# Three MLPs as half products inside the attention groups of the next query block

## The chip, the cores and the metric

The kernel runs on one core of a Trainium2 chip. The metric is the device time of one execution in microseconds (us), the median of several runs; lower is better. The core's engines work beside each other and wait for one another by semaphores: PE multiplies matrices (PEld is its loading of weights, which may lie beside a matmul), DVE (VectorE), ACT (ScalarE) and POOL (GpSimd) work elementwise, and SP issues transfers (DMA).

## The reference

One transformer layer, 2048 rows of 512 features, 32 heads of 16, and an MLP with 1792 hidden features, all in float32:

```python
def _A_ref(x, wqkv, wo):
    ...
    scores = jnp.einsum("bhqd,bhkd->bhqk", q, k) * scale
    p = _softmax(scores, axis=-1)
    o = jnp.einsum("bhqk,bhkd->bhqd", p, v)
    return (lambda x, *d: x.transpose(*d))(o, 0, 2, 1, 3).reshape(B, S, D) @ wo

def _B_ref(x, w1, w2):
    h = jnp.einsum("bsd,df->bsf", x, w1)
    h = _silu(h)
    out = jnp.einsum("bsf,fd->bsd", h, w2)
    return out

x = A_x
h = x + _A_ref(_layernorm(x, axis=-1), A_wqkv, A_wo)
h2 = h + _B_ref(_layernorm(h, axis=-1), B_w1, B_w2)
```

## The kernel before

Products are made in halves of precision: an operand is split into a high and a low fp16 part, and each product is three matmuls (high x high, low x high, high x low). So a first MLP product for 128 hidden features and 512 rows is 12 matmuls (4 chunks of features by 3), and the second product of 128 rows is 42 (14 chunks of hidden features by 3).

The 2048 queries are worked in four query blocks of 512, and a block in eight items of four heads each, so there are 32 items. An item has 16 groups, one for each 128 keys: 512 groups in all, numbered g in the main loop (L1347). A group makes four score matmuls, one for each head, of 128 keys by 512 queries; an operand is 64 rows deep, 48 of features in three parts and 16 that subtract the row's maximum. Two of the four heads lie on the upper 64 rows of the PE's array and two on the lower 64, so a matmul on one half can run beside one on the other. `scores` (L462) puts each result through the exponential on ACT into an SBUF tile. `values` (L856) multiplies the exponentials of a group with the values, four heads beside each other in float32, two groups behind (`LAG`), and adds them up in one bank of PSUM over the 16 groups; then the sum is copied out (`finish_item`, L874).

The maximum of a row must be known before the scores of its item begin. `maximum` (L285) makes a matmul of 128 queries by 512 keys, 48 rows deep, and a reduce on DVE; an item needs 64 of them, the kernel 2048. `maxima` (L1324) decides how many of them stand in a group, by how far ahead the next items' maxima are due and by a most of three, and the loop puts each behind a score of the other half. `singles` and `burst` (L443, L438) put them elsewhere: three amid an output product, and six or four at a time, as pairs of banks with one reduce for two, between the products of an MLP.

PSUM has eight banks. In attention, four are for scores (`st`), three for single maxima (`sm`), used in turn, and one for the values.

After the last item of a query block come its output product and normalization (`output`, L1184), in the second half of the item that follows, and then, ahead of the second item (`marks`), the whole MLP (`finish_block` and `mlp`, L1204 and L1118): 14 first products of 12 whole matmuls, each through SiLU on ACT, and then the second products. This is done for the first three query blocks. The last block's MLP comes at the end (`finish_last`).

What sets the order: every engine's instructions keep the order in which the program issues them, and transfers are issued by SP in that order too.

Of the kernel before, what the change touches and what calls it, by code (L numbers as in the profile page):

```python
# [20 lines left out]
P = 128  # L21
# [22 lines left out]
SPLIT = 12  # L44
MX = 2.0 ** 15
# [3 lines left out]
PTS = 16  # L49

EARLY = 8
# [13 lines left out]
WAIT = 2  # L65
JOINT = 2
AHEAD = 4
# [4 lines left out]
BESIDE = (138, 138, 110)  # L72
OUTPUT = 8

# [16 lines left out]
def attention_mlp_kernel(ctx: ExitStack, tc: tile.TileContext, x, wqkv, wo, w1, w2, out):  # L91
# [5 lines left out]
    def mm(*a, **k):  # L97
        tc.keep_in_program_order(nc.tensor.matmul(*a, **k))  # L98
# [12 lines left out]
    def act(fn, *a, **k):  # L111
        pin(getattr(nc.scalar, fn)(*a, **k))  # L112
# [80 lines left out]
    factors = const.tile([P, 14], F32, name="factors")  # L193
    sigma, inverse = factors[:, :4], factors[:, 4:8]
    w1_s, w2_s, wo_s, o_s = (sigma[:, n:n + 1] for n in range(4))
    h_f, g_s, out_f, wo_f, o_minus, o_twice = (factors[:, n:n + 1] for n in range(8, 14))
# [141 lines left out]
    def place_far(piece):  # L338
# [4 lines left out]
        issue = dma_beside if at["beside"] else dma  # L343
# [27 lines left out]
    at = {"item": 0, "done": 0, "half": 0, "step": 0, "due": 0, "attention": False, "group": None, "ready": 0, "next": 0, "blocks": True, "beside": False}  # L371
# [21 lines left out]
    def found_maxima(piece):  # L393
        g = at["group"]
        marked = g is not None and g + 1 in marks
        if g is None or marked or piece[1] is None and start_of(piece) - g > FAR:
            soon(WAIT + 1 if g is None or marked else CALM, place_far, piece)
            finish_max(piece, marked)
            return
# [55 lines left out]
    pts, den, pools = {}, {}, []  # L455
    taken = iter(range(10 ** 6))

    def pt_tile(name, dtype=F32):
        pool_of = pools[next(taken) % PTS >= EARLY]
        return pool_of.tile([P, 512], dtype, tag="pt", name=name)  # L460

    def scores(g, k, kind="st"):  # L462
# [7 lines left out]
        pts[g, k] = pt_tile("pt")  # L470
        act("activation", pts[g, k], ps, AF.Exp, scale=qk_f)


    with ExitStack() as pa:
        pb = pa.enter_context(ExitStack())
        lay_out(sm=range(5), st=range(5, 8))
        wp = pa.enter_context(tc.tile_pool(name="wp", bufs=1))
        wvp = pb.enter_context(tc.tile_pool(name="wvp", bufs=1, side="right"))
        xp = pa.enter_context(tc.tile_pool(name="xp", bufs=3))
# [34 lines left out]
        def square_rest(u):  # L514

            n = u - 7
            if 0 <= n < len(pieces):
                square_into(staged[n % 2], staged[n % 2], n)
# [931 lines left out]
```

## Time and profile before

| | us |
|---|---|
| time, median of 3 runs | 1593.08 (1592.78 to 1593.82) |
| span of the profiled execution | 1591.2 |
| PE busy | 1579.5 |
| DVE busy | 1386.9 |
| ACT busy | 1205.0 |
| POOL busy | 484.8 |

The profiled execution is listed with its span, the time from its first instruction to its last; its own time is not listed beside the runs, and the median of the runs is 1.9 us above the span. Times in rows count from the start of the span. The ends of matmuls are modelled: a matmul of 512 columns is listed with 0.38 us, though the next may start 0.22 us later, so starts are read and not ends. The granted clock of the PE is 1.00 in all of the stretches, which is its upper level (2.4 GHz).

### The profile page before, as it was taken

The numbers are of one execution on the slowest core, as the hardware profiler recorded it, in microseconds if no ns is written. First come the engines' busy times: TensorE is split into PE (matmuls) and PEld (weight loads), VectorE is DVE, ScalarE is ACT, GpSimd is POOL, SyncE is SP. The second block draws the span as 40 slices with busy tenths as digits, with TensorE's granted clock in tenths as the row PEclk, the third lists the DMA queues.
The fourth block names the chain that finished last, engine by engine and source line by source line (L and its number), as shares of the span: only waits on it lengthen the run. The fifth ranks groups of instructions, "written<-read, shape, count | busy, mean of one in ns | idle before, by whom it ended". The sixth has DMA issues, their size and how long they took to land. (4 is left out here: it accounts for less than half of the span.)

```text
span 1591.2 us, 28420 instructions
## 1 busy us (share of the span) xinstructions
PE 1579.5 (99%) x10476; PEld 471.7 (30%) x10476; DVE 1386.9 (87%) x2045; ACT 1205.0 (76%) x2384; POOL 484.8 (30%) x764
## 2 busy tenths in 40 slices
PE   9999999999999999999999999999999999999999
PEld 6434222222223322222224322222224322222254
DVE  7999999999998889999988889999986889998432
ACT  6545799999964179999973179999974189999732
POOL 5643544544446101211146101211146101211200
PEclk9999999999999999999999999999999999999999
DMA  6667533443443511121243521112143511100232
GB/s 216 174 177 221 136 86 91 113 119 86 116 100 102 157 47 35 38 51 44 50 102 101 152 53 34 39 41 53 48 104 108 159 40 37 34 12 22 74 87 73
DMA packets 124099, 140.29 MB, mean 88 GB/s; under 512 B 41808, under 2 KB 78736, under 8 KB 123960
## 3 DMA queue, kind: packets, MB, share of 16 engines
q1 hardware_dynamic: 117744, 128.34, 30.5%
q10 hardware_dynamic: 6216, 10.15, 2.3%
q8 instruction: 82, 1.34, 0.4%
q14 instruction: 57, 0.47, 0.1%
HBM read 104.68 MB, written 24.85 MB: 81 GB/s over the span
## 5 line engine op out<-in xcount | busy, mean ns | idle before, releaser
L112 ACT ACTIVATE pt<-ps 128x512 f32<-128x512 f32 x2048 | 1009.3, 611 | 154.4 <-PE ps L98 154.0
L301 DVE TENSOR_REDUCE mx<-ps 128x1 f32<-128x512 f32 x1470 | 925.1, 684 | 48.2 <-PE ps L98 20.3
L98 PE MATMUL ps<-pt,va 128*17 128x512 f32 x4096 | 537.5, 598 | 1.1
L98 PE MATMUL ps<-qs,ks 64*128 64x512 f16 x2048 | 530.9, 379 | 1.5 <-DMA qs<-mn 0.4
L98 PE MATMUL ps<-ks,qs 48*128 48x512 f16 x2048 | 495.4, 380 | 2.6 <-ACT pvs L112 1.1
L299 DVE TENSOR_REDUCE mx<-ps 128x2 f32<-128x1024 f32 x289 | 334.9, 1219 | 43.8 <-PE ps L98 42.5
L98 PEld LDWEIGHTS <-ks 64*128 64x128 f16 x2048 | 149.3, 95 | 549.2 <-issue 432.5
L105 POOL TENSOR_TENSOR ri<-rc,minus 128x16 f32<-128x16 f32 x31 | 90.7, 2926 | 242.5 <-DMA rc<-dn 192.3
L98 PE MATMUL ps<-w,gh 128*128 128x512 f16 (+1 forms) x678 | 154.4, 378 | 0.0
L98 PE MATMUL ps<-hts,w 128*128 128x512 f16 (+1 forms) x708 | 153.3, 369 | 0.0
L98 PEld LDWEIGHTS <-qs 48*128 48x128 f16 x2048 | 126.1, 94 | 77.5 <-issue 61.3
L98 PEld LDWEIGHTS ps<-pt,va 128*17 128x17 f32 x4096 | 69.0, 95 | 225.7 <-issue 205.4
L112 ACT ACTIVATE g<-ps,factors 128x512 f32<-128x512 f32 x56 | 38.4, 686 | 125.0 <-PE ps L98 95.7
L105 POOL TENSOR_TENSOR mx<-mx 128x32 f32<-128x32 f32 x52 | 12.6, 241 | 386.4 <-DVE mx L301 379.8
L98 PEld LDWEIGHTS <-w 128*128 128x128 f16 x708 | 66.5, 98 | 78.6 <-issue 10.2
L98 PEld LDWEIGHTS <-gh 128*128 128x128 f16 x678 | 63.1, 98 | 82.9 <-issue 13.7
L112 ACT ACTIVATE ks<-ps 128x512 f32<-128x512 f32 x30 | 17.9, 598 | 50.5 <-PE ps L98 45.1
L115 DVE SCALAR_TENSOR_TENSOR gh<-g,factors,gh 128x512 f16<-128x512 f32 x14 | 10.5, 751 | 52.1 <-ACT gh L112 52.1
L105 POOL TENSOR_TENSOR sl<-ks,sh 128x512 f16<-128x512 f32 x30 | 34.7, 1157 | 51.5 <-ACT sh L112 38.1
L105 POOL TENSOR_TENSOR gh<-g,gh 128x512 f16<-128x512 f32 x42 | 48.6, 1156 | 3.5
L105 POOL TENSOR_TENSOR ot<-ot,den 128x512 f32<-128x512 f32 (+1 forms) x16 | 20.4, 1273 | 84.4 <-DMA den<-dr 75.8
L98 PE MATMUL ps<-xth,wqk_h 128*128 128x512 f16 x120 | 45.8, 381 | 0.0
(155 smaller groups left out, 919.7 us busy)
## 6 DMA issues: line engine op xcount, KB each, us to landing
w<-w2d SPq DMA_DIRECT2D x98, 256.0 KB
ks<-kd SPq DMA_DIRECT2D x120, 192.0 KB
w<-w1d SPq DMA_DIRECT2D x56, 256.0 KB
ks<-in_B_w_dram ACTq DMA_DIRECT2D x28, 256.0 KB
w<-in_B_w_dram SPq DMA_DIRECT2D x28, 256.0 KB
qs<-qd SPq DMA_DIRECT2D x128, 48.0 KB
kd<-sh SPq DMA_DIRECT2D x16, 256.0 KB
qd<-sh SPq DMA_DIRECT2D x16, 256.0 KB
```

Of the source, the lines that this page charges most:

```text
L98: tc.keep_in_program_order(nc.tensor.matmul(*a, **k))
L105: tc.keep_in_program_order(getattr(nc.gpsimd, op)(*a, **k))
L112: pin(getattr(nc.scalar, fn)(*a, **k))
L115: pin(getattr(nc.vector, fn)(*a, **k))
L299: pin(nc.vector.tensor_reduce(of, space[:, n:n + 2, :], axis=AX.X, op=ALU.max))
L301: pin(nc.vector.tensor_reduce(of[:, j:j + 1], space[:, n, :], axis=AX.X, op=ALU.max))
```

## The change

The MLPs of the first three query blocks are no longer made in one piece. From the second group after a mark on, 112 groups (110 in the last of the three) each take a share of them. A matmul of 128 rows is cut into two of 64 rows, one on the upper and one on the lower half of the array, which add into one bank of PSUM (bank 3, taken from the scores, which keep three). A group makes six halves (seven in the last chain of some 14 groups) on one half of the array, and its four scores all on the other half: an even group makes the scores of two heads for itself and the next group, an odd group those of the other two heads for the group before and itself. Four groups make a first product, 14 a second product of 128 rows. A half product waits for the last exponential of the group before (`after`). In these groups the values are one group behind, and four maxima stand in a group (five or three where an item's maxima fall late); the SiLU is made from a tanh on ACT and four steps on POOL; the sum of the second product is scaled on ACT and added on POOL. The weights of the second product are loaded once for each 128 rows, so four times for a block.

Elsewhere, an ordinary group may have four maxima, the output product of each 128 rows has three maxima amid it in all blocks, and the values' sums are copied out by ACT from the second query block on. Bursts of pairs now stand only in the projections ahead of the loop.

```diff
--- before.py
+++ after.py
 SPLIT = 12
+SPACING = 4
 MX = 2.0 ** 15
 
 
 LAG = 2
-PTS = 16
-
-EARLY = 8
+PTS = 12
...
+AHEAD = 6
+
 JOINT = 2
-AHEAD = 4
+MORE = 3
 FAR = 8
 CALM = 4
 
 
-BESIDE = (138, 138, 110)
...
+LEAD = 7
...
-BURSTS_1 = ({f: 6 for f in range(FC) if f not in (6, 13)},) * 2 + ({f: 6 for f in range(FC) if f % 3 != 1},)
-BURSTS_2 = 12, 12, 10
-SPAN_2 = 12 * (FC - 2) - 3
-
-MORE = 2, 2, 0
...
+    def after(ins, earlier):
+
+        tc.add_manual_dep(ins.ins, earlier.ins.name, mybir.DependencyInfo(
+            mybir.DependencyClass.Sync, mybir.DependencyReason.DATA), reason="row halves in one bank")
...
 def scores(g, k, kind="st"):
...
-        pts[g, k] = pt_tile("pt")
-        act("activation", pts[g, k], ps, AF.Exp, scale=qk_f)
+        def weigh():
+            pts[g, k] = pt_tile("pt")
+            return act("activation", pts[g, k], ps, AF.Exp, scale=qk_f)
+
+        return weigh
...
-        elif i in FIRSTS:
+        elif i < FIRSTS[0]:
+            dve("tensor_copy", pvs, pv)
+        else:
             act("copy", pvs, pv)
-        else:
-            dve("tensor_copy", pvs, pv)
         if i == LAST:
...
-    def mlp(b):
...
+    weights_of = [*(("w1", f) for f in range(FC)), *(("w2", f) for _ in range(4) for f in range(FC))]
+    wanted = []
+
+    def want(n):
+        for _ in range(min(n, len(wanted))):
+            load_weights(*wanted.pop(0))
+
+    def take(kind, f):
+        want(1)
+        return ws.pop((kind, f))
+
+    def first_of(f):
+        w1h, w1l = (w.rearrange("p (c n) -> p c n", n=P) for w in take("w1", f))
+        for c in range(DC):
+            for w, x in ((w1h, hth), (w1l, hth), (w1h, htl)):
+                yield w[:, c, :], x[:, c, :]
+
+    def second_of(t):
+        rows = slice(t * P, (t + 1) * P)
         for f in range(FC):
-            tick()
-            next_weights()
-            w1h, w1l = (w.rearrange("p (c n) -> p c n", n=P) for w in ws.pop(("w1", f)))
-            ps = space[:, f % 2, :]
-            n = BURSTS_1[b].get(f, 0)
-            if f == 0:
-                burst(n, 4, 6, 2)
-                n = 0
-            weave(product(ps, lambda c: w1h[:, c, :], lambda c: w1l[:, c, :],
-                          lambda c: hth[:, c, :], lambda c: htl[:, c, :], DC),
-                  {6: lambda: burst(n, 4, 6, 2)} if n else {})
-            gates.append(gate(ps, "pool"))
-
-        act("activation", small.tile([P, 1], F32, name="sw"), ident[:, :1], AF.Exp)
-        acc = [space[:, n, :] for n in range(4)]
-        positions = {SPAN_2 * (n + 1) // BURSTS_2[b]: n for n in range(BURSTS_2[b])}
-
-        def insert(k):
-            half = 12 * FC // 2
-            pairs = (4, 6)
-            if not (half - 12 < k < half + 12 or k == SPAN_2):
-                pairs = (2 if k < half else 0), 4, 6
-            burst(2 * len(pairs), *pairs)
-
-        k = 0
-        for part in range(2):
-            for f in range(0, FC - 4 * part, 2):
-                at["beside"] = part == 0 or f < 4
-                tick()
-                next_weights()
-                next_weights()
-                for _ in pair_seconds(b, acc, (2 * part, 2 * part + 1), f, gates):
-                    k += 1
-                    if k in positions:
-                        insert(k)
-        for _ in range(2):
-            tick()
-            next_weights()
-            next_weights()
-
-        def scores_in(*ring):
-            lay_out(sm=ring)
-            some_scores(4)
-
-        last_seconds(b, acc, gates[-4:], {6: lambda: scores_in(0, 1, 4, 5), 18: lambda: scores_in(6, 7, 4, 5)}, (2, 3))
-        lay_out(sm=attention_banks[:3])
+            w2h, w2l = take("w2", f)
+            for side, w in ((0, w2h), (1, w2h), (0, w2l)):
+                yield gates[:, f, side, rows], w
+
+    def end_first(f, ps):
+        z = zp.tile([P, 512], F32, name="g")
+        act("mul", z, ps, h_f)
+
+        def bend():
+            t = zp.tile([P, 512], F32, name="t", tag="oh")
+            act("activation", t, z, AF.Tanh, scale=0.5)
+            pool("tensor_scalar", t, t, 1.0, g_half, op0=ALU.add, op1=ALU.mult)
+            pool("tensor_tensor", t, t, z, ALU.mult)
+            pool("tensor_copy", gates[:, f, 0], t)
+            low(gates[:, f, 1], t, gates[:, f, 0], "pool")
+
+        soon(2, bend)
...
+    def end_second(b, t, ps):
+        z = zp.tile([P, 512], F32, name="g")
+        act("mul", z, ps, out_f)
...
+    chains, current = [], {}
+
+    def begin_mlp(b):
+        chains.extend((3 * DC, 6, first_of(f), lambda ps, f=f: end_first(f, ps)) for f in range(FC))
+        chains.extend((3 * FC, 7 if 4 * b + t == KC - 5 else 6, second_of(t), lambda ps, t=t: end_second(b, t, ps)) for t in range(4))
+
+    def half_product(j):
+        if j == 0:
+            current["open"].append(next(current["of"]))
+        lhs, rhs = current["open"][current["half"][j] - current["gone"]]
+        if j:
+            current["open"].pop(0)
+            current["gone"] += 1
+        r = slice(64 * j, 64 * j + 64)
+        ins = mm(space[:, 3, :], lhs[r], rhs[r], start=current["half"] == [0, 0],
+                 stop=current["half"][1] == current["count"] - 1)
+        if "fence" in current:
+            after(ins, current.pop("fence"))
+        current["half"][j] += 1
+
+    def beside_products(g, n):
+
+        if not current:
+            count, share, of, end = chains.pop(0)
+            current.update(count=count, share=share, of=of, end=end, half=[0, 0], open=[], gone=0)
+        side = g % 2
+        heads = [(x, k) for x in (g - side, g - side + 1) for k in range(4) if head(x, k)[1] != side]
+        i, found, left = next_item(), [0, 0], [0, 0]
+        if i < ITEMS:
+            left = [len(todo[i, j]) for j in range(2)]
+        count = current["count"] - current["half"][0] if side == 0 else current["half"][0] - current["half"][1]
+        count = min(current["share"], count)
+        for _ in range(min(n, sum(left))):
+            j = 1 - side
+            if 4 + found[j] > count + found[side] or found[j] == left[j]:
+                j = side
+            if found[j] == left[j]:
+                j = 1 - j
+            found[j] += 1
+        other = [("max", 1 - side)] * found[1 - side]
+        other = [step for m, of in enumerate(heads) for step in [("score", of), *other[m:m + 1]]]
+        same = [("max", side)] * found[side]
+        same[1:1] = [("half", side)] * count
+        short = len(same) - len(other)
+        if short > 0:
+            other[-1:-1] = [("none", 0)] * short
+        waiting = []
+        for m in range(max(len(other), len(same))):
+            for kind, x in same[m:m + 1] + other[m:m + 1]:
+                if kind == "score":
+                    waiting.append(scores(*x))
+                    if len(waiting) < 4:
+                        waiting[-1]()
+                elif kind == "max":
+                    one_max(x)
+                elif kind == "half":
+                    half_product(x)
+        if current["half"][1] == current["count"]:
+            current["end"](space[:, 3, :])
+            current.clear()
+            waiting[3]()
+        else:
+            current["fence"] = waiting[3]()
...
-            weave(project_rows(n, ps), {6: lambda: singles(3)} if n < MORE[b] else {})
+            weave(project_rows(n, ps), {6: lambda: singles(MORE)})
...
-    def finish_block(b, pending):
-
-        act("activation", small.tile([P, 1], F32, name="sw"), ident[:, :1], AF.Silu)
-        load_weights("w1", 4)
-        for g in pending:
-            values(g)
-        mlp(b)
...
+    beside = {g for m in marks for g in range(m + 2, min(groups, m + 2 + 4 * FC + 4 * FC))}
+    fixed = {**{8 * KC * b + c: 3 + MORE * (OUTPUT < c <= OUTPUT + 4) for b in range(1, NB) for c in range(2, KC + 2)},
+             **{g: 4 for g in beside}}
+    before = [sum(n for x, n in fixed.items() if x < g) for g in range(groups + 1)]
+    free = [sum(x not in fixed for x in range(g)) for g in range(groups + 1)]
+
...
+        if g in beside:
+            at["due"] = 0
+            most = 4 - late_now + (64 + 4 * (g + LEAD) > at["done"])
+            return max(0, min(most, ready - at["done"]))
...
+        if g in fixed:
+            rate = 3
...
-        most = 2 if at["step"] in late or c == JOINT and i and i - 1 not in FIRSTS else 3
+        most = 2 if late_now or c == JOINT and 0 < i <= FIRSTS[0] else 4
...
-            finish_block(i // 8 - 1, (g - 2, g - 1))
+            begin_mlp(i // 8 - 1)
+        if (g in beside) != (g - 1 in beside):
+            lay_out(st=range(3 if g in beside else 4))
...
+        if g in beside:
+            beside_products(g, n)
+        else:
...
-        if g - LAG >= 0 and not (g in marks or g - 1 in marks):
-            values(g - LAG)
+        while done <= g - (1 if g in beside else LAG):
+            values(done)
+            done += 1
```

The rest of the diff: buffers change their pools and places (12 tiles for exponentials instead of 16, room for all gates of a block), the factors are computed in two parts, and finding a maximum that is far from due takes a path on POOL everywhere.

The order on the PE in a group of the third query block's items, before: `ks` and `qs` are keys and queries; a row that writes from `ks` with the weights `qs` is a maximum, one from `qs` with the weights `ks` a score; `pt,va` are values.

```order
L98 MATMUL ps<-pt,va 17x512 x4
L98 LDWEIGHTS ks_99
L98 MATMUL ps<-qs_100,ks_99 128x512
L98 LDWEIGHTS qs_106
L98 MATMUL ps<-ks_105,qs_106 128x512
L98 LDWEIGHTS ks_99
L98 MATMUL ps<-qs_100,ks_99 128x512
L98 LDWEIGHTS qs_106
L98 MATMUL ps<-ks_105,qs_106 128x512
L98 LDWEIGHTS ks_99
L98 MATMUL ps<-qs_100,ks_99 128x512
```

The start of a group beside the MLP in the changed kernel, in the same notation; `hts,w` is a half of a first product.

```order
L97 MATMUL ps<-pt,va 17x512 x4
L97 LDWEIGHTS qs_108
L97 MATMUL ps<-ks_107,qs_108 128x512
L97 LDWEIGHTS ks_105
L97 MATMUL ps<-qs_106,ks_105 128x512
L97 LDWEIGHTS w
L97 MATMUL ps<-hts,w 128x512
L97 LDWEIGHTS qs_108
L97 MATMUL ps<-ks_107,qs_108 128x512
L97 LDWEIGHTS w
L97 MATMUL ps<-hts,w 128x512
L97 LDWEIGHTS ks_105
```

Before, such a group is score, maximum, score, maximum, score, maximum, score. Now it is maximum, score, half, maximum, half, score, half, maximum, half, score, half, maximum, half, score: 14 matmuls between two values blocks instead of seven, and the whole products of the MLP stand nowhere else.

The end of a group near the beginning of the first query block, before, on the PE:

```order
L98 LDWEIGHTS ks_99
L98 MATMUL ps<-qs_100,ks_99 128x512
L98 LDWEIGHTS qs_106
L98 MATMUL ps<-ks_105,qs_106 128x512
L98 LDWEIGHTS ks_99
L98 MATMUL ps<-qs_100,ks_99 128x512
L98 MATMUL ps<-pt,va 17x512 x4
```

And the end of the same group in the changed kernel:

```order
L97 LDWEIGHTS ks_99
L97 MATMUL ps<-qs_100,ks_99 128x512
L97 LDWEIGHTS qs_106
L97 MATMUL ps<-ks_105,qs_106 128x512
L97 LDWEIGHTS ks_99
L97 MATMUL ps<-qs_100,ks_99 128x512
L97 LDWEIGHTS qs_106
L97 MATMUL ps<-ks_105,qs_106 128x512
L97 MATMUL ps<-pt,va 17x512 x4
```

A fourth maximum now stands behind the last score, ahead of the values. Of the 128 groups after the first, 30 have four maxima, 11 have two and 87 three; before, none has more than three.

## Rows read from the trace of the kernel before

**Rows 1.** The page: busy us, share of the span, instructions of each engine.
```profile
PE 1579.5 (99%) x10476; PEld 471.7 (30%) x10476; DVE 1386.9 (87%) x2045; ACT 1205.0 (76%) x2384; POOL 484.8 (30%) x764
```

**Rows 2.** Windows: stretch, length, busy PE PEld DVE ACT POOL (instructions), clock, DMA, GB/s.
```profile
179.40:431.80 252.40, 251.56 (x1913) 56.03 (x1912) 240.64 (x391) 251.99 (x515) 123.54 (x185) 1.00 0.41 108
431.80:472.60 40.80, 40.52 (x265) 10.81 (x267) 37.42 (x64) 30.47 (x62) 16.68 (x24) 1.00 0.42 84
472.60:571.20 98.60, 97.88 (x503) 37.77 (x498) 83.83 (x81) 28.00 (x44) 35.94 (x59) 1.00 0.42 119
571.20:791.10 219.90, 219.65 (x1674) 48.86 (x1673) 210.83 (x343) 219.79 (x449) 36.75 (x68) 1.00 0.19 44
791.10:1150.80 359.70, 358.19 (x2438) 97.51 (x2437) 332.42 (x486) 278.37 (x553) 87.95 (x145) 1.00 0.27 69
1150.80:1499.80 349.00, 347.36 (x2337) 94.61 (x2341) 288.49 (x431) 274.10 (x542) 87.06 (x139) 1.00 0.26 67
```

**Rows 3.** Timeline of the PE, one group: start us, duration, instruction, count.
```profile
701.84 0.39 PE L98 MATMUL ps<-qs,ks 64*128 64x512 f16 x1
701.84 0.60 PE L98 MATMUL ps<-ks,qs 48*128 48x512 f16 x2
...
702.50 0.38 PE L98 MATMUL ps<-qs,ks 64*128 64x512 f16 x1
702.81 1.05 PE L98 MATMUL ps<-pt,va 128*17 128x512 f32 x8
703.79 0.39 PE L98 MATMUL ps<-qs,ks 64*128 64x512 f16 x1
```

**Rows 4.** Timeline of ACT and DVE, the first exponential and reduce of that group.
```profile
702.26 0.60 ACT L112 ACTIVATE pt<-ps 128x512 f32<-128x512 f32 x1
...
702.29 0.69 DVE L301 TENSOR_REDUCE mx<-ps 128x1 f32<-128x512 f32 x1
```

**Rows 5.** Timeline of PE and DVE, a maximum that waits for its bank.
```profile
466.89 1.28 DVE L301 TENSOR_REDUCE mx<-ps 128x1 f32<-128x512 f32 x2
...
468.23 0.37 PE L98 MATMUL ps<-ks,qs 48*128 48x512 f16 x1
```

**Rows 6.** Timeline of the PE in the first MLP: bursts and first products.
```profile
479.17 0.82 PE L98 MATMUL ps<-ks,qs 48*128 48x512 f16 x6
479.93 2.76 PE L98 MATMUL ps<-hts,w 128*128 128x512 f16 x12
482.62 0.94 PE L98 MATMUL ps<-ks,qs 48*128 48x512 f16 x6
```

**Rows 7.** Timeline of the PE, the values behind three output groups.
```profile
449.35 1.05 PE L98 MATMUL ps<-pt,va 128*17 128x512 f32 x8
...
454.74 1.05 PE L98 MATMUL ps<-pt,va 128*17 128x512 f32 x8
...
459.48 1.05 PE L98 MATMUL ps<-pt,va 128*17 128x512 f32 x8
```

**Rows 8.** Timeline of the PE near the loop's end: values behind groups without maxima.
```profile
1479.45 1.05 PE L98 MATMUL ps<-pt,va 128*17 128x512 f32 x8
...
1481.41 1.05 PE L98 MATMUL ps<-pt,va 128*17 128x512 f32 x8
...
1498.08 2.77 PE L98 MATMUL ps<-pt,va 128*17 128x512 f32 x24
```

**Rows 9.** The page's groups: busy us, mean ns of one, idle before.
```profile
L301 DVE TENSOR_REDUCE mx<-ps 128x1 f32<-128x512 f32 x1470 | 925.1, 684 | 48.2 <-PE ps L98 20.3
...
L98 PEld LDWEIGHTS <-ks 64*128 64x128 f16 x2048 | 149.3, 95 | 549.2 <-issue 432.5
...
L112 ACT ACTIVATE g<-ps,factors 128x512 f32<-128x512 f32 x56 | 38.4, 686 | 125.0 <-PE ps L98 95.7
```

**Rows 10.** Windows, a stretch of the first MLP's second products, columns as above.
```profile
520.00:560.00 40.00, 39.82 (x203) 15.60 (x202) 35.43 (x34) 3.46 (x5) 5.32 (x8) 1.00 0.57 159
```

More of the change, by code (lines that the diff above doesn't have):

```diff
@@ L342, in place_far @@
         dve("transpose", mt, split.pop(piece))
-        issue = dma_beside if at["beside"] else dma
+        issue = dma
         for b in range(4):
@@ L370, in attention_mlp_kernel @@
     END = 64 * ITEMS
-    at = {"item": 0, "done": 0, "half": 0, "step": 0, "due": 0, "attention": False, "group": None, "ready": 0, "next": 0, "blocks": True, "beside": False}
+    at = {"item": 0, "done": 0, "half": 0, "step": 0, "due": 0, "attention": False, "group": None, "ready": 0, "next": 0, "blocks": True}
     agenda, late = {}, {}
@@ new lines, in idle, with turn_high @@
+    def idle(n):
+        ps = bank()
+        for c in range(n):
+            tr(ps[:, columns(c % 4)], ident, ident)
+    def turn_high(b, t):
+        ps = bank("sm").rearrange("p (c n) -> p c n", n=P)
+        high = xth[b] if b else xth0
+        for c in range(4):
+            tr(ps[:, c, :], xts[b][:, t, c * P:(c + 1) * P], ident)
+        act("copy", high[:, :, columns(t)], ps)
+        return ps
+    idle(20)
+    found = [statistics(xts[0][:, t, :], LN) for t in range(2)]
+    turned, ps_vs = [], []
@@ new lines, in first_rows, with first_products @@
+    def first_rows(t):
+        normalize(xts[0][:, t, :], xts[0][:, t, :], *found[t])
+        turned.append(turn_high(0, t))
+    def first_products(t, *chunks):
+        if t == len(ps_vs):
+            ps_vs.append(bank("st" if t < 3 else "sm"))
+        for c in chunks:
+            mm(ps_vs[t], xth0[:, c, columns(t)], wv0_h[:, c, :], start=c == 0, stop=False)
+    first_rows(0)
+    idle(4)
+    found.append(statistics(xts[0][:, 2, :], LN))
+    act("copy", wv0_h[:, 0, :], raw_v[:, 0, :])
@@ new lines, in attention_mlp_kernel @@
+    for h in range(4):
+        loads[3 + h] = (load_k, 3, h), (load_q, 3, h)
+    BESIDE_T = {6: lambda: begin_scores(3), 11: lambda: begin_scores(3)}, {1: lambda: (begin_scores(2), singles(2))}
+    at["blocks"] = False
+    for g in range(1, NG // 2):
+        for m, (b, key) in enumerate([(b, 1) for b in range(NB)] + [(b, 0) for b in range(NB)]):
+            tick()
+            if g == 1 and m < 2:
+                fixed_rows(2 + m)
+            n = 8 * g + m - 12
+            square_rest(n + 24)
+            if n == 15:
+                measure_rest()
+            beside = {BESIDE_A1[m]: 6} if g == 1 and m < len(BESIDE_A1) else BESIDE_A
+            if n >= 18:
+                beside = BESIDE_T[n - 18]
+            project_qk(b, 2 * g + key, beside, True)
+            for load, i, h in loads.get(n, ()):
+                load(i, h)
@@ L1420, in attention_mlp_kernel @@
     agenda.clear()
-    finish_last((groups - 2, groups - 1))
+    finish_last(range(done, groups))
 _INS = ["A_x", "A_wqkv", "A_wo", "B_w1", "B_w2"]
```

747 lines of the change are left out of this document (347 added, 400 removed).

## The prediction

> **What bounds the kernel now.** The page comes first: the PE is called busy for 99% of the span, DVE for 87%, ACT for 76% [rows 1]. A PE that is busy all the time on the page says little, so the windows by stage come next [rows 2]. In an attention stretch (571.2 to 791.1) ACT is busy 219.79 of 219.90 us with 449 instructions, 0.49 us each. In the MLP stretch that follows the first block (472.6 to 571.2) ACT is busy 28.00 of 98.60 us, while the PE runs without a break. So the kernel alternates between attention, where three engines are nearly full, and MLPs, where ACT is idle.
>
> The timeline of one ordinary group shows how full the PE is [rows 3]. Scores and maxima go in pairs, one on each half of the array's rows. Four such slots start 0.22 us apart (701.84 to 702.50 is three of them), the values start 0.31 after the last slot, and the next group starts 0.98 after the values. Together 1.96 us, in which there is no hole: 0.31 is one slot of 0.22 and a turnaround of 0.09, and of 0.98 a values block proper is 0.86 (three of them back to back last 2.77 with their tail) [rows 8]. ACT needs 4 x 0.49 = 1.96 as well (a group with four scores and no maxima, two slots, is no faster: 1479.45 to 1481.41 [rows 8]). DVE needs 3 x 0.60: two reduces in a row take 1.28 [rows 5], one 0.68 [rows 9], so they start 0.60 apart.
>
> **The change, part by part.** The sum is made on the profiled execution, whose span is 1591.2 us; the median of the timed runs is 1593.1, so 1.9 lie around it. Counts of instructions are from the order of the changed kernel.
>
> *One fact carries most terms: a maximum may start only when its bank is free.* The maxima have three banks, used in turn. In the ordinary group the first maximum starts at 701.84 and its reduce at 702.29, 0.45 later, and lasts 0.69 [rows 3, 4]. A reduce that ends at 468.17 lets the next maximum start at 468.23, 0.06 later, with the PE standing until then [rows 5]. So the fourth maximum of a group starts at the earliest 0.45 + 0.69 + 0.06 = 1.20 us after the first. With three maxima in a group, as now, this never shows.
>
> *First 128 groups.* The new pace gives four maxima to 31 of the groups (with the one ahead of the loop), where now none has more than three; 11 have two. The fourth would go in the slot at 0.66; it goes at 1.20, and the values after it. 31 x 0.54 = +16.7. Groups with two give nothing back, because ACT's 1.96 holds them. The seven copies of finished values on DVE, which fall ahead of such groups, add some 0.2 each: +1.5. Bounds: 0 (if the surplus is worked off later; DVE's total of 403 x 0.60 = 242 fits in 252.4 [rows 2]) to +20.
>
> *Groups beside the MLP: 112 + 112 + 110.* Each gets six half products, its four scores and four maxima: 14 matmuls of half the rows, seven slots. That would be 7 x 0.22 + 0.09 + 0.98 = 2.62 us. The fourth maximum stands in the sixth slot, at 1.11 if nothing holds it; the bank lets it go at 1.20. The last score follows 0.22 later, the values 0.31 after that, the next group 0.98 later: 2.71. I take 2.71. DVE needs 4 x 0.60 = 2.40 and ACT 1.96 plus at most 0.36 (two more activations in four groups, 0.69 each [rows 9]), so both are covered. The new wait of a half product for the exponential of the group before costs nothing here: an exponential starts 0.42 after its score (701.84 to 702.26) and lasts 0.60 [rows 3, 4], so the last one starts by 1.9 in its group and ends by 2.5, and the first half product of the next group comes at 2.93. Weight loads hide as they do now (below). The weights of the second product are now fetched four times: two loads of 256 KB in 5.4 us is 97 GB/s, on top of attention's 44 [rows 2]; the present MLP moved 159 GB/s with the PE at 39.82 of 40 [rows 10], so they are in time, five loads ahead.
>
> *Output groups.* Now 18 maxima stand among the four of them, then 24 (23 in the last block). DVE is the full one there: 37.42 of 40.80 in that stretch [rows 2]. Three more maxima cost the PE 0.65 in a group (449.35 to 454.74 against 454.74 to 459.48 [rows 7]); on DVE six cost 6 x 0.60 = +3.6. Bounds 1.3 (two groups at 0.65) to 4.5; I take 3.6, as DVE is the nearer row.
>
> *Where blocks 2 and 3 find their maxima late* (the lead is seven groups), an item has one group with a transpose and one with five maxima: the fifth waits for the second reduce, 0.45 + 0.60 + 0.69 + 0.06 = 1.80, so 3.09 instead of 2.71, and 0.1 for the transpose: 0.5 an item.
>
> *The last 23 groups* have no maxima but six or seven halves beside four scores, six or seven slots: 2.5 and 2.63, some 59.1 in all, against 1.96 each now. The first half product comes first in its group, so there the wait for the exponential takes 0.1.
>
> The blocks, from one block's end to the next [rows 2]:
> Block 1 now: 40.8 + 98.6 + 219.9 = 359.3. After: six ordinary groups 12.3 (one with four maxima), the output groups and the three behind them 27.4 + 3.6 = 31.0 (40.8 less six groups and two values blocks, plus the above), two ordinary 3.9, 112 x 2.71 = 303.5, one more values block as the lag shrinks 0.9: 351.6, so -7.7.
> Block 2 now 359.7. After: a double group without values between 3.9, five ordinary 9.8, 31.0, 3.9, 0.9, 303.5, seven late items 3.5: 356.5, so -3.2.
> Block 3 now 349.0. After: 3.9 + 9.8 + 31.3 + 3.9 + 0.9, 87 groups with maxima 240.0 (71 at 2.71, ten with five maxima at 3.08, six with a transpose at 2.8), 23 without 59.1 and the last values 0.9: 349.8, so +0.8.
>
> Projections and the last block's MLP keep their instructions: 0. The gates by tanh lie on ACT and POOL, off the path; the table loads that go are in the MLP stretches already counted. Sum: 16.7 + 1.5 - 7.7 - 3.2 + 0.8 = +8.1, so 1593.1 + 8.1, about 1601 us. The MLP's 98.6 us becomes 112 x 0.75 = 84: the half products need the same PE time as whole ones, and what is won is only that maxima no longer have slots and turnarounds of their own (a burst of six now takes 0.76, and the twelve products behind it 2.69, of which 0.10 is turnaround [rows 6]).
>
> **A rule against it.** In the ordinary group each half of the rows takes matmul after matmul 0.22 us apart, each with a weight load of 0.095 on the same half [rows 3, 9]; whole products go 0.216 apart [rows 6], so at most 0.006 of a load is seen. The Trainium skill (TensorE: Matmul & The Clock Gate, Part 3, The mechanism) says that a weight load overlaps running matmuls only where the row group differs. By it six half products in a row on one half would each show their load: 7 x 0.095 = 0.67 a group, 334 groups, +222 us. By the rows the load is hidden, and I go by them.
>
> **The rivals.**
> *A: the bank wait does not bind.* Place: the sixth slot of the groups beside the MLP. If the reduce is free sooner than 1.11, the group takes 2.62: 334 x 0.09 = 30 less, 1571, faster. It decides from a group of 2.68 downwards (8.1 / 334 = 0.024). For it: DVE has 0.3 us of slack in each such group. Against: slack does not shorten one reduce's own 1.20. If the 31 groups of the first block also pay nothing, 1555.
> *B: ACT gets behind, and the half product's wait for the exponential bites.* Values one group behind, two more activations a chain and the copies of finished values moved to ACT make its order tighter: in odd groups the values need exponentials of the same group (the second is done by 0.42 + 0.49 + 0.60 + 0.06 = 1.57, the values come at 1.73, a margin of 0.16). If 0.1 a group is lost: 334 x 0.1 = +33, 1634; at 0.2, 1668.
> *C: the weights come late*, since SP issues them in line with waits of other transfers. One wait of 5 us in each of 84 chain ends is hidden by five loads ahead; if half the second-product groups (56 a block) lost 0.5 us, +42, 1643.
> *D: the weight loads show*, as the rule has it: some 1820.
>
> **How the numbers follow.** Forecast (2.71 a group, within some 10 us of 1601) 0.54; A 0.24; B 0.13; C 0.06; D 0.03. About 0.2% (3 us) is what a measurement can tell from no change. Of the forecast's 0.54 some 0.08 lie within 3 us of 1593, 0.07 below and 0.39 above. With A all faster but 0.03, and B, C, D all slower: faster 0.28, same 0.11, slower 0.61. The range leaves out the low end of A (1555) and the high ends of B, C and D: 1568 to 1632; the likeliest case alone is 1590 to 1612.
>
> **What would show it.** Right: values blocks 2.7 us apart beside the MLP, the PE standing about 0.1 before the fourth maximum with DVE's reduce as releaser, DVE idle 0.3 in such a group, ACT idle 0.4 or more; in the first 128 groups some gaps of 2.5 among those of 1.96, and that stretch near 270 instead of 252.4. Wrong: 2.62 or less (A), values or half products released by ACT (B), half products released by DMA (C), slots 0.3 apart (D), or an early stretch that stays at 252.

## The result: 0.45% slower, as a sum of larger terms of both signs

The changed kernel takes 1599.99 us (median of four runs, 1599.64 to 1601.64) against 1593.15 for the kernel before on the same chip (1592.78 to 1593.82). The ratio is 1.0045, with a 95% interval of 1.0030 to 1.0059. The profiled execution spans 1597.8 us where before had 1591.2, so the traces differ by 6.6, nearly what the medians do (6.8), and the account below is made on the traces.

The page's first line of engines, of the changed kernel, against [rows 1]:

```profile
PE 1574.8 (99%) x11495; PEld 474.3 (30%) x11495; DVE 1375.0 (86%) x2211; ACT 1237.7 (77%) x2404; POOL 565.1 (35%) x803
```

The PE is called busy 4.7 us less than before in a span that is 6.6 longer, so its holes grew by 11.3 us; the next views show where. The windows by stage (columns as in [rows 2]; the cuts are at the starts of values blocks, as they are there: the first, the one 128 groups later and so on):

```profile
184.30:455.00 270.70, 265.38 (x1944) 57.67 (x1946) 256.53 (x419) 254.83 (x510) 122.69 (x183) 0.99 0.36 99
455.00:803.10 348.10, 346.49 (x2760) 95.72 (x2761) 322.40 (x532) 285.49 (x555) 118.22 (x180) 1.00 0.34 91
803.10:1156.30 353.20, 351.11 (x2776) 97.78 (x2777) 326.09 (x543) 288.05 (x560) 110.49 (x141) 1.00 0.33 91
1156.30:1505.40 349.10, 346.40 (x2671) 96.68 (x2672) 276.09 (x465) 284.36 (x552) 112.05 (x143) 1.00 0.31 86
1505.40:1597.80 92.40, 88.48 (x462) 44.08 (x456) 27.74 (x48) 25.04 (x39) 4.47 (x9) 1.00 0.27 83
```

Against [rows 2], in which block 1 is the second to fourth row together (359.3) and the first values come at 179.4: the start +4.9, the first 128 groups +18.3, block 1 -11.2, block 2 -6.5, block 3 +0.1, what follows it +1.0 (92.4 against 1591.2 - 1499.8 = 91.4). The sum is +6.6.

*Beside the MLP* the values blocks come 2.675 us apart (2.73 in the first group of an item). The timeline of one such group, PE and DVE (start us, duration, instruction; the PE's rows of weight loads are left out):

```profile
594.25 1.05 PE L97 MATMUL ps<-pt,va 128*17 128x512 f32 x8
595.24 0.39 PE L97 MATMUL ps<-ks,qs 48*128 48x512 f16 x1
...
595.66 2.48 DVE L307 TENSOR_REDUCE mx<-ps 128x1 f32<-128x512 f32 x4 [0.19 <-PE ps L97]
...
596.12 0.38 PE L97 MATMUL ps<-hts,w 64*128 64x512 f16 x1
596.12 0.38 PE L97 MATMUL ps<-qs,ks 64*128 64x512 f16 x1
596.33 0.38 PE L97 MATMUL ps<-hts,w 64*128 64x512 f16 x1
596.41 0.37 PE L97 MATMUL ps<-ks,qs 48*128 48x512 f16 x1
...
596.93 1.05 PE L97 MATMUL ps<-pt,va 128*17 128x512 f32 x8
```

The rows of the PE `ks,qs` are maxima, `qs,ks` scores, `hts,w` half products. The halves go 0.215 apart on their side of the array (596.12, 596.33), without a gap. On the other side a score starts at 596.12, and the next in that queue, the fourth maximum, at 596.41 and not at 596.34: 0.07 is lost. This hole has no mark in brackets, because the half at 596.33 covers it and the engine as a whole is never idle; it is seen only by following one side. From the first maximum to the fourth it is 1.17, in 274 of the groups. DVE was idle 0.19 before these four reduces, where the prediction asked for 0.3.

*In the first 128 groups* a group with four maxima shows the same wait in the open (PE and DVE):

```profile
220.06 0.60 PE L97 MATMUL ps<-ks,qs 48*128 48x512 f16 x2
...
220.51 2.48 DVE L307 TENSOR_REDUCE mx<-ps 128x1 f32<-128x512 f32 x4 [0.21 <-PE ps L97]
220.72 0.38 PE L97 MATMUL ps<-qs,ks 64*128 64x512 f16 x1
221.25 0.37 PE L97 MATMUL ps<-ks,qs 48*128 48x512 f16 x1 [0.16 <-DVE mx L307]
```

The first maximum starts at 220.06, the fourth at 221.25, and the PE stands 0.16 with DVE's reduce as releaser (the rest of the hole is the end of the score's 0.38). Twenty-nine gaps between values blocks are 2.49 there, the others 1.87 to 2.21 but for the first, 3.56.

*The start*, which the prediction put at 0 (POOL, DVE and PE):

```profile
179.44 1.16 POOL L104 TENSOR_TENSOR sl<-ks,sh 128x512 f16<-128x512 f32 x1 [2.30 <-issue]
...
180.68 0.23 POOL L104 TENSOR_SCALAR norms<-norms 128x1 f32<-128x1 f32 x1
181.00 0.57 POOL L104 TENSOR_TENSOR norms<-norms,expos 128x1 f32<-128x1 f32 x1
...
181.60 0.15 DVE L121 TENSOR_SCALAR factors<-norms 128x1 f32<-128x1 f32 x1 [4.16 <-POOL norms L104]
...
183.81 0.58 PE L97 MATMUL ps<-ks,qs 48*128 48x512 f16 x1 [4.50 <-DVE mx L307]
```

`set_output_factors` raises the fourth norm to its power on POOL, behind the last projection's `sl`. DVE's first factor waits 4.16 us for it, and the reduces of the first maxima are queued behind that factor; the PE waits 4.50 for a bank. Before, this power was taken with the other three, long before.

**The theory** that goes into the experiments: a group's fourth maximum can't start before its bank's first reduce is done (0.424 + 0.692 + 0.053 = 1.169 us after the first maximum: its reduce starts, lasts, and the bank is free), and this sets the pace of the groups beside the MLP and of those with four maxima ahead of it; the start's 4.9 is the norm on POOL. The rivals: the PE needs its 2.67 for fourteen matmuls and the values whatever their order, or DVE, which reduces without much pause, sets the pace.

### The profile page after: what moved, and what is told of

It is laid out like the page before. It is cut to its first block, busy times and chain, and to the rows that moved or that the text cites. A ratio compares the mean times of both kernels' runs of the same rounds, so it can differ in the third digit from the quotient of the medians.

```text
span 1597.8 us, 31074 instructions
## 1 busy us (share of the span) xinstructions
PE 1574.8 (99%) x11495; PEld 474.3 (30%) x11495; DVE 1375.0 (86%) x2211; ACT 1237.7 (77%) x2404; POOL 565.1 (35%) x803
## 4 chain that ended last, share of the span: by engine, by line
PE 90%; DVE 6%; ACT 2%; issue 1%; POOL 1%; POOLq 0%; DVEq 0%; ACTq 0%
PE ps L97 89%; DVE mx L307 3%; ACT pt L111 2%; PE ps L100 1%; DVE mx L305 1%; DVE ot L121 0%; DVE st L121 0%; DVE w L121 0%; DVE pvs L121 0%; POOL wv_l L104 0%; POOL sl L104 0%; DVE ks L121 0%; DVE xtl L121 0%; DVE mv L121 0%; POOL rs L104 0%
## 5 line engine op out<-in xcount | busy, mean ns | idle before, releaser
L307 DVE TENSOR_REDUCE mx<-ps 128x1 f32<-128x512 f32 x1842 | 1145.8, 683 | 87.0 <-PE ps L97 80.3
L97 PE MATMUL ps<-qs,ks 64*128 64x512 f16 x2048 | 685.2, 379 | 1.1 <-ACT pt L111 1.0
L97 PE MATMUL ps<-ks,qs 48*128 48x512 f16 x2048 | 628.3, 379 | 13.5 <-DVE mx L307 11.6
L97 PE MATMUL ps<-hts,w 64*128 64x512 f16 (+2 forms) x1212 | 283.6, 370 | 0.6 <-ACT pt L111 0.6
L97 PE MATMUL ps<-w,gates 64*128 64x512 f16 x1008 | 244.7, 376 | 0.5
L97 PEld LDWEIGHTS <-w 64*128 64x128 f16 (+1 forms) x1212 | 114.0, 94 | 130.2 <-issue 34.5
L97 PEld LDWEIGHTS <-gates 64*128 64x128 f16 x1008 | 92.3, 94 | 130.1 <-issue 28.6
L305 DVE TENSOR_REDUCE mx<-ps 128x2 f32<-128x1024 f32 x103 | 119.2, 1217 | 4.1 <-PE ps L97 3.5
L104 POOL TENSOR_TENSOR t<-t,g 128x512 f32<-128x512 f32 x42 | 53.5, 1275 | 3.5
L104 POOL TENSOR_TENSOR gates<-t,gates 128x512 f16<-128x512 f32 x42 | 48.6, 1158 | 3.4
```

Source lines behind the costliest of these rows:

```text
L97: return tc.keep_in_program_order(nc.tensor.matmul(*a, **k))
L104: tc.keep_in_program_order(getattr(nc.gpsimd, op)(*a, **k))
L305: pin(nc.vector.tensor_reduce(of, space[:, n:n + 2, :], axis=AX.X, op=ALU.max))
L307: pin(nc.vector.tensor_reduce(of[:, j:j + 1], space[:, n, :], axis=AX.X, op=ALU.max))
```

## The experiments

All start from the changed kernel (1600.0; span 1597.8), one edit each unless said. Times are medians beside runs of the kernel before on the same chip, which gave 1593.4 for the first four and 1593.2 for the last three, against 1593.15 beside the changed kernel, so a difference from the changed kernel is good to some 0.3.

**1. The fourth maximum a slot later.**

```
 in beside_products, where the halves' side has one maximum and the scores' side three, with six halves:
+    other[-2:] = other[-1], other[-2]      # the last score ahead of the last maximum
...
     current["fence"] = waiting[3]()
+    if swap: current["fence"] = reduce     # of that last maximum
```

> One edit: in the groups beside the MLP with four maxima and six halves, the last score and the fourth maximum change places, so the fourth maximum stands in the seventh slot (at 6 x 0.2155 = 1.293 us after the first) instead of the sixth (1.08); the next group's first half then waits for the reduce of that maximum instead of the last exponential. Bank-wait theory (the fourth maximum can't start before 0.424 + 0.692 + 0.053 = 1.169 after the first): the wait of 0.09 goes, such a group takes 2.585 to 2.60 instead of 2.675; 277 groups x 0.075 to 0.09 = 21 to 25 us less, so 1575 to 1579. Rival 1 (the array needs 2.67 for these fourteen matmuls and the values, whatever their order): no change, 1600 within 2. Rival 2 (DVE is the bound of such a group: four reduces, the reduce moved 0.12 later): the wait moves to the next group's maxima, 1595 to 1605. Rival 3 (the new wait for the reduce delays halves): slower than 1600.

Measured: 1603.97 (1603.49 to 1604.22), ratio to before 1.0067 (1.0050 to 1.0084), 4 us slower than the change. The values blocks (PE):

```profile
595.36 1.05 PE L97 MATMUL ps<-pt,va 128*17 128x512 f32 x8
...
597.97 1.05 PE L97 MATMUL ps<-pt,va 128*17 128x512 f32 x8
...
600.72 1.05 PE L97 MATMUL ps<-pt,va 128*17 128x512 f32 x8
```

They come 2.61 and 2.75 apart in turn, 2.68 in the mean. The timeline of a slow group tells why (DVE's seven reduces are those of two groups in one row):

```profile
591.41 4.50 DVE L307 TENSOR_REDUCE mx<-ps 128x1 f32<-128x512 f32 x7 [0.29 <-PE ps L97]
...
593.60 0.39 PE L97 MATMUL ps<-ks,qs 48*128 48x512 f16 x1
...
593.95 0.09 PEld L97 LDWEIGHTS <-w 64*128 64x128 f16 x1 [0.26 <-DVE mx L307]
```

The weights of the group's first half product are loaded, and it starts, 0.35 behind the group's first maximum instead of 0.22, released by DVE. Rival 3, then, decided: the four reduces run back to back, 0.60 apart, so the last one ends 0.42 + 3 x 0.60 + 0.68 = 2.90 after the group's first maximum, not 0.42 + 0.69 after its own, as I had reckoned for the new wait. The next group's first half wanted to go at 2.61 + 0.22 = 2.83. The experiment removed one wait and made another of the same size; the 4 us are lost elsewhere (the blocks take 0.9 to 1.3 more each, at their seams among others, and the first 128 groups, which the edit doesn't touch, 0.6). That half of the groups do take 2.61 speaks against "the PE needs 2.67", but a better arrangement was needed to show it (5).

**2. The fourth norm early.**

```
 in measure_rest:
-    pool("tensor_scalar", norms[:, :3], norms[:, :3], 1e-30, ...); pool("tensor_tensor", norms[:, :3], ..., ALU.pow)
+    pool("tensor_scalar", norms, norms, 1e-30, ...); pool("tensor_tensor", norms, norms, expos, ALU.pow)
 in set_output_factors: the two lines for norms[:, 3:] go
```

> One edit: the power of the fourth norm is taken with the other three, as in the kernel before, and not when the attention starts. If the 4.16 us that DVE waited for POOL's norms at 181.60 cost the start 4.9 us: the first values 4.9 earlier and the total 4.9 less, about 1595.1. Rival (the start is held by something else, such as the transfers of the first items, and the norms only end last): less than 2 us gained, 1598 or more.

Measured: 1594.66 (1594.32 to 1595.09), ratio to before 1.0007 (0.9998 to 1.0017). DVE and PE at the start:

```profile
177.52 0.14 DVE L121 TENSOR_SCALAR factors<-norms 128x1 f32<-128x1 f32 x1
...
179.70 0.37 PE L97 MATMUL ps<-ks,qs 48*128 48x512 f16 x1 [0.25 <-DVE mx L307]
180.01 1.05 PE L97 MATMUL ps<-pt,va 128*17 128x512 f32 x8
```

The factor starts at 177.52 instead of 181.60, and the first values at 180.0 instead of 184.3. The gain is 5.3, of which 4.3 lie ahead of the first values and 1.1 in the first 128 groups, 269.6 now; what that 1.1 was is in the last section. So two instructions that take 0.80 us in sum were 5.3 of the 6.8 us by which the change loses. The other 0.6 of the start's 4.9 is not theirs: the fourth maximum of the group ahead of the first values stands there at 179.70, with a wait for its bank. With three maxima there as well (experiment 6) the first values come at 179.39, as in the kernel before.

**3. Threes for twos.**

```
-    most = 2 if late_now or c == JOINT and 0 < i <= FIRSTS[0] else 4
+    most = 3 if late_now or c == JOINT and 0 < i <= FIRSTS[0] or g < 64 else 4
```

> One edit, to the pace: groups that were held to two maxima may have three, and the first 64 groups never more than three. The groups with four maxima outside the MLPs fall from 39 to 25; groups with five stay 17. If each fourth maximum costs 0.53 (2.49 against 1.96) and the third in a group that had two costs nothing: 14 x 0.53 = 7.4 less, 1592.6; the first 128 groups 10 x 0.53 = 5.3 less, 265.4 instead of 270.7. Rival (the third maximum collides there with the transposes and copies on DVE that the hold to two made room for): half of that or nothing, 1596 to 1600.

Measured: 1596.02 (1595.10 to 1596.97), ratio 1.0016 (1.0006 to 1.0026): 4.0 less, where 7.4 were expected. The first 128 groups take 268.6, so 2.1 less and not 5.3; blocks 1 and 2 give 0.5 and 0.6, the start 0.9. The rival had half of the story. Behind a joint between two items, where the edit puts the third maximum (DVE and PE):

```profile
216.48 0.68 DVE L121 COPY pvs<-ps 128x512 f32<-128x512 f32 x1
...
217.08 1.87 DVE L307 TENSOR_REDUCE mx<-ps 128x1 f32<-128x512 f32 x3
...
219.00 0.37 PE L97 MATMUL ps<-ks,qs 48*128 48x512 f16 x1
```

The copy of the finished values delays three reduces, and a maximum of the next group goes at 219.00, 0.35 later than its slot. Such a group, with three maxima instead of four, takes 2.31 and not 1.96, five times (+1.7). Two others behind a joint keep their four and take 2.69 instead of 2.49 (+0.4), and the second group of all, behind the stall at the start that this run still has, takes 2.70 instead of 1.96 (+0.7). Of the ten groups that no longer have four, one lies ahead of the first values (0.5 of the start's 0.9). In sum this is about the 3.2 that is missing. A maximum more is free on DVE as a sum, not at a joint.

**4. Fewer maxima amid output products.**

```
-MORE = 3
+MORE = 2
```

> One edit: two more maxima instead of three amid each output product (20 in the four output groups instead of 24). Elsewhere the pace makes up for it: 42 groups with four maxima among the first 128 instead of 31, no groups with five beside the second MLP instead of seven, seven threes fewer there. If a maximum amid output products costs DVE's 0.60 and each surplus four 0.53: output 12 x 0.60 = -7.2, first groups 11 x 0.53 = +5.8, beside the second MLP 14 groups, half 0.41 less and half as long as before = -2.9: in sum -4.3, 1595.7. Rival (the third maximum amid an output product is hidden, as the PE waits there for other things): output groups within 0.5 of 29.97 us a block as now, total +2 to +3, about 1602.5.

Measured: 1600.27 (1599.93 to 1600.68), ratio 1.0044 (1.0027 to 1.0061): no difference from the change. The windows of the first 128 groups and of the three blocks:

```profile
184.50:461.70 277.20, 270.27 (x1951) 58.12 (x1950) 262.70 (x430) 256.37 (x510) 122.15 (x183) 0.99 0.35 96
461.70:810.30 348.60, 346.35 (x2754) 95.86 (x2754) 320.79 (x528) 285.84 (x556) 119.27 (x186) 1.00 0.34 91
810.30:1157.90 347.60, 346.74 (x2762) 96.63 (x2760) 322.06 (x531) 287.53 (x560) 121.88 (x189) 1.00 0.35 93
1157.90:1505.40 347.50, 345.32 (x2667) 96.62 (x2667) 273.30 (x462) 283.81 (x552) 112.08 (x143) 1.00 0.32 87
```

The first 128 groups +6.5 (expected +5.8), block 1 +0.5, block 2 -5.6, block 3 -1.6. Neither theory gave the sum. The maxima amid output products are not hidden: four output groups take 5.2 each in the second and third block (but for one), against 5.4 to 6.6. But a maximum that is not found there is found in a group with four, 0.59 each, and the pace, which plans for all items ahead, takes eleven more of them before the first MLP. So whether a maximum is cheaper in one place can't be read from that place alone: it depends on where the pace puts what is taken away there.

**5. The order that avoids both waits**, in even groups only, where the values need no exponential of the same group.

```
 in beside_products:
+    swap = side == 0 and found == [1, 3] and count == 6
+    if swap:
+        same.append(same.pop(0))                       # six halves, then this side's maximum
+        other[:6] = [step for m in range(0, 6, 2) for step in (other[m + 1], other[m])]   # maximum, score
...
     current["fence"] = waiting[3]()
+    if swap: current["fence"] = exp                    # of the third score, which follows the sixth half
```

> One edit, in even groups beside the MLP with four maxima and six halves: the three maxima of the scores' side of the array go ahead of their scores (slots 1, 3, 5), and the fourth, of the halves' side, goes last on its side, behind the sixth half (slot 7). So 6 x 0.2155 = 1.293 us lie between the first and the fourth maximum, and the next group's first half waits for the third score's exponential, which ends before it. Odd groups stay as they are and are the control in the same trace. Bank-wait theory (1.169 at least from the first maximum to the fourth): even groups 2.585 to 2.61, odd ones 2.675 as now; some 139 even groups x 0.07 to 0.09 = 10 to 12 us less, so 1588 to 1590. Rival 1 (PE bound: seven slots and the values need 2.67): even groups stay at 2.67, 1600. Rival 2 (DVE bound: four reduces end 2.90 after the first maximum, so whatever is won in an even group is lost in the odd group behind it): odd groups 2.74, total 1600.

Measured: 1593.98 (1593.01 to 1595.16), ratio to before 1.0005 (0.9995 to 1.0014): 6.0 less than the change, and the same as before. Three values blocks behind each other (PE), the first interval an even group, with its first and its fourth maximum, the second an odd one:

```profile
594.45 0.62 PE L97 MATMUL ps<-pt,va 128*17 128x512 f32 x4
...
595.44 0.39 PE L97 MATMUL ps<-ks,qs 48*128 48x512 f16 x1
...
596.74 0.38 PE L97 MATMUL ps<-ks,qs 48*128 48x512 f16 x1
...
597.06 1.05 PE L97 MATMUL ps<-pt,va 128*17 128x512 f32 x8
...
599.74 0.62 PE L97 MATMUL ps<-pt,va 128*17 128x512 f32 x4
```

Even groups take 2.61, odd ones 2.68, in the same trace, with the same fourteen matmuls and the same four reduces. The fourth maximum of the even group goes 1.30 behind the first, in its slot and with its bank free; in the odd one it still goes at 1.17. So the 0.07 is the fourth maximum's wait for its bank, and neither rival holds: the PE doesn't need it, and DVE doesn't take it back. The changed kernel's own trace agrees: its one group of six halves, four scores and three maxima without a transpose takes 2.614 (516.64 to 519.25). The gain is half of the 11 expected: of the 139 groups with the new order 116 gain 0.065, not 0.075 to 0.09, and all together 7.5. Of this 1.0 is given back at the seams, where the first group of two MLPs takes 3.23 instead of 2.98 and most items' first ones 2.76 instead of 2.73, and 0.7 at the start and in the first two groups behind it, which the edit doesn't touch. In the odd groups I found no order without a wait: their values need the second exponential of the same group. To drop the half product's wait alone would leave two row halves writing one bank unordered; it was not tried.

**6. The three edits together** (2, 3 and the order of even groups).

> Three edits together: the even groups' new order, the fourth norm taken early (-5.3 alone), and the pace with threes for twos (-4.0 alone). If the three causes are separate, their gains add: 1600.0 - 11 - 5.3 - 4.0 = about 1580, below the kernel before (1593.4). Rival (they share a cause, the pace of DVE): less than the sum, 1585 or more.

Measured: 1583.55 (1583.39 to 1585.24), ratio to before 0.9939 (0.9922 to 0.9955). The sum of the single gains is 6.0 + 5.3 + 4.0 = 15.3, the gain together 16.4: the gains add up, as separate causes would, and the rival, one cause behind them, is out. This beats the kernel before by 0.6%.

**7. One block with fewer maxima amid its output products**, on top of 6.

```
-MORE = 3
+MORE = 3, 3, 2
```

> The three edits, and two maxima instead of three amid each output product of the third block alone. The pace then gives three groups more with four maxima ahead of the MLPs (+3 x 0.55 = 1.6), and beside the second MLP only groups of four instead of seven with five and seven with three (-7 x 0.41 = -2.9, and some 0.5 for transposes); four maxima fewer amid output products (-1.5 to -2.4). In sum some 3 to 4 us less than the three edits alone, about 1577. Rival (the output products' maxima are hidden, as the even result of the run with fewer in all blocks may say): within 1 us of the three edits.

Measured: 1581.91 (1580.96 to 1582.83), ratio to before 0.9927 (0.9910 to 0.9943). That is 1.6 less than 6, and the two sets of runs don't overlap; 3 to 4 were expected. The windows of the three blocks:

```profile
448.10:796.00 347.90, 345.33 (x2757) 101.86 (x2757) 323.31 (x532) 284.48 (x555) 119.35 (x186) 1.00 0.33 91
796.00:1143.50 347.50, 345.16 (x2767) 102.67 (x2765) 324.37 (x536) 286.85 (x560) 120.61 (x183) 1.00 0.34 93
1143.50:1488.90 345.40, 343.11 (x2666) 100.44 (x2666) 273.60 (x462) 283.17 (x552) 112.11 (x143) 1.00 0.31 87
```

Blocks 2 and 3 gain 3.0 and 4.0 on run 6 (350.5 and 349.4 there), about what was expected. The first 128 groups lose 1.7 (268.4 for 266.7), as expected, and block 1 loses 3.0 (344.9), which was not: its first output group took 7.58 instead of 5.41. POOL shows why:

```profile
463.21 0.24 POOL L104 TENSOR_TENSOR mx<-mx 128x32 f32<-128x32 f32 x1
...
465.98 0.29 POOL L104 CAST oh<-ot 128x128 f16<-128x128 f32 x1
...
466.32 1.11 PE L97 MATMUL ps<-wo_h,oh 128*128 128x512 f16 x2 [1.31 <-POOL oh L104]
```

The nine steps that finish an item's maxima (463.21 to 466.03) now stand on POOL ahead of the cast of `oh`, the operand of the output product, and the PE waits 1.31 for it. Behind that the granted clock is 0.50 from 468 to 470, and the next group takes 6.45 where run 6 has 6.09. Run 6 has such a stretch elsewhere: behind the second MLP its clock is 0.50 from 1146 to 1148, and a group there takes 3.40, where run 7 has 1.96. So 1.4 of block 3's 4.0 is this stretch, not fewer maxima. Of the executions of both runs, those listed with a mean clock of 1.000 took 1583.4 to 1583.6 (three, run 6) and 1581.0 to 1581.2 (two, run 7), 2.4 apart. This is the best version of the study.

## Why the prediction was right

The likeliest case came, at 1600.0 against 1601, within its own range. Its steps:

- **The bank wait** (the fact that carried most terms): right. 1.17 us from the first maximum to the fourth where 1.20 was said, with DVE's reduce as the marked releaser in the first 128 groups (beside the MLP the hole has no mark), and shown by the even and odd groups of one trace. Rival A, that it does not bind, is out.
- **First 128 groups** +18.2 said, +18.3 measured. 29 gaps of 2.49 are 15.4; what the prediction gave to the seven copies on DVE (1.5) is in truth for the most part the groups behind the fours (2.01 to 2.13) and the slow first group. The agreement is in part luck: 1.1 of the 18.3 is the stall at the start (last section), and the 31st group with four, ahead of the first values, is in the 18.2 but not in the 18.3.
- **Beside the MLP** 2.71 said, 2.675 measured: the term was mis-sized by 0.035. The 0.45 from a maximum's start to its reduce was read from an ordinary group [rows 3, 4]; beside the MLP it is 0.42 (595.24 to 595.66), and the slot itself is 0.215 and not 0.22. (Without the wait the prediction's sum is 2.61, not 2.62 as written there; the reordered even groups take 2.61.) Over 110 groups this is 3.9, and blocks 1 and 2 came out 3.5 and 3.3 below the forecast (-11.2 for -7.7, -6.5 for -3.2).
- **Output groups** 31.0 said for the four and the three behind them, 29.97 measured in block 1 (5.41, 5.38, 6.57, 5.83, 1.96, 2.57 and 2.25), from 27.4.
- **Late items** +0.5 said, +0.35 measured (2.62 and 3.08 for two groups of 2.675).
- **The last 23 groups** 59.1 said, 61.2 measured (1443.29 to 1504.45): most gaps are 2.56 to 2.64, with two of 3.2, where four transposes of finished values stand beside the halves, and one of 2.85. The 87 groups with maxima ahead of them took 237.7 where 240.0 was said, so the two errors cancel in block 3.
- **The start** 0 said, +4.9 measured, of which 4.3 are the norm (5.3 with its aftermath) and 0.6 the 31st group with four. This step failed, and experiment 2 shows its cause. The prediction put the stretch ahead of the first values at nothing, because the projections keep their instructions. That the factors are computed in two parts was known; it did not ask which queue the second part stands in and who is behind it.
- **The last group of an MLP**, priced at 3.9 with the group behind it, took 4.53 and 4.71. The chain's closing activation is issued ahead of the group's fourth exponential (ACT and PE):

```profile
803.46 0.71 ACT L111 ACTIVATE g<-ps,factors 128x512 f32<-128x512 f32 x1
804.03 0.63 ACT L111 ACTIVATE pt<-ps 128x512 f32<-128x512 f32 x1
...
804.71 0.37 PE L97 MATMUL ps<-qs,ks 64*128 64x512 f16 x1 [0.52 <-ACT pt L111]
```

The tail's +1.0 begins in the same way: at 1504.81 a `g` stands ahead of the last exponential, and the output product follows the last values 0.7 later than before. The rest of it is not explained.

Three smaller slips don't bear on the sum: two activations of 0.69 in four groups are 0.345 a group and not 0.36; the three MLPs have 54 chains and not 84; and the bank wait does show in groups of three where DVE is late, as in [rows 5], though the prediction says that it never does.

So the total is as close as it is by errors that cancel: the three blocks came out 7.5 us lower than forecast (3.5, 3.3 and 0.7), the start and the end 5.9 higher. Rival B showed only at these seams. C did not show: the page's groups list no wait of the half products for a transfer (0.6 us for ACT in the row of the first products, which includes the last block's whole ones, and 0.5 in all in that of the second products):

```profile
L97 PE MATMUL ps<-hts,w 64*128 64x512 f16 (+2 forms) x1212 | 283.6, 370 | 0.6 <-ACT pt L111 0.6
L97 PE MATMUL ps<-w,gates 64*128 64x512 f16 x1008 | 244.7, 376 | 0.5
```

D did not show either: the halves start 0.215 apart, six in a row on one half of the rows, each with its own weight load. By the Trainium skill (TensorE: Matmul & The Clock Gate, Part 3, The mechanism) such loads would not overlap; here the measurement decides, and they do.

Where the gain went, then: the first MLP's 98.6 us are gone [rows 2], and 110 of its 112 groups beside attention pay 110 x (2.675 - 1.96) = 78.7 for it (the first two, at the seam, take 2.98 and 3.53). The 138 maxima that used to be found in that MLP have to be found elsewhere, mostly as a group's fourth, and the fourth is what costs: an ordinary group with four takes 2.49 without a single half product, so six halves beside them cost 0.185 us more.

## What to carry to other kernels

When work is packed into a loop's holes, price each group by its longest chain through a buffer ring (here three banks: matmul, reduce, free), not by the busy time of its engines; the fourth user of three buffers pays the full round trip of the first. If a wait is moved to another instruction, work out when that one ends behind everything queued ahead of it on its own engine. And when start-up code is rearranged, look at what stands behind each moved instruction on its queue: 0.8 us of it cost 5.3, and POOL's steps ahead of one cast cost the best version 1.31 of waiting.

## What was not expected of the hardware

The stall at the start cost more than its length. The windows around it in the changed kernel (the figure behind the parenthesis of POOL is the granted clock):

```profile
178.00:184.00 6.00, 1.50 (x8) 0.20 (x6) 2.15 (x9) 3.17 (x6) 3.43 (x11) 0.73 0.53 122
184.00:186.00 2.00, 2.00 (x9) 0.15 (x8) 1.54 (x3) 0.00 (x0) 0.16 (x2) 0.50 0.92 196
188.00:190.00 2.00, 1.95 (x15) 0.31 (x9) 1.99 (x5) 1.58 (x4) 1.92 (x3) 1.00 1.00 253
```

After the PE had stood for 4.50 us, the clock granted from 184 to 186 was 0.50, the lower of its two levels (1.2 GHz), and it was back at 1.00 from 188 on. The first gap between values blocks was 3.56 us. With the norm early (experiment 2) the clock stays at 1.00 there, and the first gap is 2.49 (180.01 to 182.50):

```profile
180.00:182.00 2.00, 2.00 (x16) 0.44 (x16) 1.99 (x4) 2.00 (x5) 1.81 (x7) 1.00 0.56 191
```

That is the 1.1 us which experiment 2 gained inside the first 128 groups.
